# Sliding-window attention feeding a feed-forward layer: later batches loaded in runs of four tokens, V on another queue, and a re-ordered first batch

## The chip, the cores and the metric

The kernel runs on one core of one Trainium2 chip. The metric is device time in microseconds (us). A run is called fast or slow: a slow run is one more than 1.5% above the fastest run of the same kernel.

## The reference

Eight batches of eight heads attend over 576 tokens with head size 64, each token to its neighbours within 32 positions. The result, 4608 rows of 512, goes through a two-layer feed-forward block.

```python
scores = q @ k.T / sqrt(64); mask = |i - j| <= 32          # q, k, v: (8, 8, 576, 64) float32
x = softmax(where(mask, scores, -1e9)) @ v                  # to (4608, 512)
h = relu(x @ w_in)                                          # w_in (512, 2048)
out = (s * h * h + b) @ w_out                               # w_out (2048, 512)
```

## The kernel before

The whole program is built as a graph of tasks. A planner with a table of estimated costs puts the tasks into one fixed order per engine queue (PE, ACT, DVE, Pool, and SP, which issues DMAs). On the chip each queue runs strictly in that order, with semaphore waits, so a task that waits for its input holds up everything behind it in its queue.

For batches 2 to 7, q and k come in by token: partition = token, and for each head 64 floats, so every contiguous run in memory is 256 bytes. DVE casts them to bf16 and a DMA transpose puts the head dimension on the partitions.

```python
def chunk(b, t0, n, key):                       # called for n = 256, 256, 64 tokens of each batch
    nx, np_ = (2, 128) if n == 256 else (1, n)
    for name in "qk":
        add("sp", [... e.dma_start(STG[si][0:np_, x*512:x*512+512].rearrange("p (h d) -> p h d", h=H),
              src_of[name][b, :, t0+128*x : ..., :].rearrange("h p d -> p h d")) for x in range(nx)], ...)
        add("dve", ... tensor_copy(NAT, STG) ...)                        # cast
        add("sp", [... e.dma_start(dst[:, :, ...], NAT[0:np_, x, :], transpose=True) for x in range(nx)], ...)

def load_v(b, t, key, waits=()):                # 128 tokens; runs of 256 bytes too
    add("sp", lambda e: e.dma_start(VST[0:n, t, :, :], v[b, :, 128*t:128*t+n, :].rearrange("h p d -> p h d")), ...)
def cast_v(b, t, key, eng, slack): ...          # eng is Pool for batches 1 to 7

def finish(b, u):                               # a unit is 128 tokens: reciprocal, normalise into XN, then
    if b < XPE: ...                             # XPE = 3: x transposed by PE, copied to XT by ACT
    else: ...                                   # x transposed by a DMA from XN to XT
# [cut: scores on PE, exponent on ACT, mask on DVE, weighted V on PE; the feed-forward stages s1 (w<-xt,win), s2 (o<-wout,gt)]
```

s1 and s2 are the dense work: 128x512 matmuls, four of which take about 0.86 us. Between s1 and s2, ACT applies relu and DVE squares (`gt<-r`).

The softmax here doesn't subtract the row's maximum and nothing guards it: scores larger than these inputs give would overflow.

## Time and profile before

| | before |
|---|---|
| time, median of the first 3 runs | 366.87 us (366.63 to 369.42) |
| span of the profiled run | 369.4 us |
| mean granted PE clock | 0.949 |
| PE idle, 100 to 270 us (40 us and 50 us windows) | 27.4 us |
| DMA share of 16 engines, 80 to 240 us | 0.78 |

These are lines of the page of the kernel before: the span, busy time and share of PE, PEld (weight loads), DVE, ACT and Pool; then rows of 40 slices, each digit a slice's busy share in tenths; the SP-issued DMA queue (packets, MB, share of 16 engines); and the chain of work that ended last, by engine.

```profile
span 369.4 us, 8204 instructions
PE 319.2 (86%) x3452; PEld 169.3 (46%) x3452; DVE 176.7 (48%) x376; ACT 141.7 (38%) x217; POOL 42.6 (12%) x64
...
PE   3679997979699569674999997979699999999996
...
PEclk9999999899889889995999998998989999999999
DMA  8999999967995974697669875797744111001012
...
q1 hardware_dynamic: 150624, 56.19, 66.1%
...
PE 54%; DMA 18%; SPq 17%; DVE 6%; issue 3%; ACT 1%; POOL 0%; DVEq 0%
```

PE is the busiest engine, but between the 7th and the 30th slice its row has holes, and the clock row dips at many of them. The Trainium skill ("TensorE: Matmul & The Clock Gate", Part 1) says that an idle PE falls back to half its clock. The trace agrees: after a wait of 7.8 us that ended at 171.4 us, four dense matmuls took 1.82 us instead of 0.86. No other engine is near full either, so the chain of waits must be read. It spends 17% of the span in SP's queue (SPq) and 18% in DMA flight.

From the chain of the kernel before in order of time (start, us, what):

```profile
121.27 0.90 SPq L421
...
125.90 1.14 SPq L463
...
127.09 2.00 SPq L463
...
129.13 1.88 SPq L588
...
131.05 2.36 DMA xt<-xn
...
133.44 0.70 DVE xn L572
```

Six load issues of 0.9 to 2.0 us, three of which are shown, stand in SP's queue ahead of one xt transpose, which frees the buffer that the next normalisation (`xn`) waits for. That is head-of-line blocking.

How fast the DMAs move seems to depend on the runs; these two windows differ in more than that, and `runs_256` below tests it. Columns: the window, busy us (and count) of PE, PEld, DVE, ACT, POOL, then clock, DMA share, GB/s; the first window moves weights in 2 KB runs, the second mostly q, k and v in 256-byte runs.

```profile
23.00:27.00 4.00, 3.51 (x83) 2.96 (x84) 2.06 (x6) 0.84 (x2) 1.04 (x1) 1.00 1.03 370
120.00:130.00 10.00, 6.08 (x66) 2.70 (x65) 5.41 (x12) 2.98 (x5) 1.61 (x2) 0.83 1.26 221
```

The waits of the kernel before (engine, line, what it waited for; total us, times, longest):

```profile
POOL vb L428 <- DMA vst<-in_v_dram: 199.1, 33, 22.9
...
DVE nat L470 <- DMA stg<-in_q_dram: 29.9, 9, 6.2
...
DVE xn L572 <- DMA xt<-xn: 23.3, 10, 5.3
...
PE avn L550 <- DMA qt<-nat: 7.8, 1, 7.8
```

### The profile page before, as it was taken

What the parts mean: (1) busy time and instruction counts of PE and PEld (TensorE: products, weight loads), DVE (VectorE), ACT (ScalarE), POOL (GpSimd) and SP (SyncE); (2) the same over time, 40 slices, a digit from 0 to 9 for tenths busy, and PEclk for the clock granted to TensorE, in tenths of its full rate; (3) what the DMA queues carried; (4) which work ended last, traced back from release to release, by engine and by line L of the source; (5) the groups of instructions that cost most, each with busy time, mean ns of one, the idle gap of its engine ahead of it and who ended that gap; (6) DMA issues with size and microseconds to landing.
All of it is one profiled execution on the core that took longest, in us unless ns stands there. A gap on an engine that the chain in (4) does not pass through costs nothing.

```text
span 369.4 us, 8204 instructions
## 1 busy us (share of the span) xinstructions
PE 319.2 (86%) x3452; PEld 169.3 (46%) x3452; DVE 176.7 (48%) x376; ACT 141.7 (38%) x217; POOL 42.6 (12%) x64
## 2 busy tenths in 40 slices
PE   3679997979699569674999997979699999999996
PEld 3459886645344223332444443434244444444442
DVE  3557875556444543442556256355265453333321
ACT  3555463456236232431444433523234443333300
POOL 3223551200110110011100110010100000000000
PEclk9999999899889889995999998998989999999999
DMA  8999999967995974697669875797744111001012
GB/s 263 245 358 357 245 287 225 158 128 151 205 155 135 226 151 96 134 219 146 142 115 199 180 167 122 148 187 161 155 112 121 46 44 67 28 30 58 31 57 85
DMA packets 150661, 56.71 MB, mean 154 GB/s; under 512 B 137312, under 2 KB 142432, under 8 KB 150624
## 3 DMA queue, kind: packets, MB, share of 16 engines
q1 hardware_dynamic: 150624, 56.19, 66.1%
q8 instruction: 27, 0.44, 0.6%
q14 instruction: 10, 0.08, 0.1%
HBM read 36.70 MB, written 9.44 MB: 125 GB/s over the span
## 4 chain that ended last, share of the span: by engine, by line
PE 54%; DMA 18%; SPq 17%; DVE 6%; issue 3%; ACT 1%; POOL 0%; DVEq 0%
PE o L730 25%; PE w L711 23%; SPq L463 6%; DMA xt<-xn 4%; DMA stg<-in_moe_w_out_dram 3%; DMA stg<-in_q_dram 3%; PE avn L550 3%; SPq L421 3%; SPq L588 2%; SPq L475 2%; DMA out_dram<-outs 2%; DMA vst<-in_v_dram 2%; DMA qt<-nat 2%; PE sc L498 2%; DVE ex L523 1%
## 5 line engine op out<-in xcount | busy, mean ns | idle before, releaser
L711 PE MATMUL w<-xt,win 128*128 128x512 bf16 (+2 forms) x704 | 152.4, 354 | 1.4 <-DMA xt<-xn 1.4
L730 PE MATMUL o<-wout,gt 128*128 128x512 bf16 (+1 forms) x640 | 151.7, 371 | 1.6 <-DVE outs L743 1.4
L718 ACT ACTIVATE r<-w 128x512 bf16<-128x512 f32 x144 | 85.9, 597 | 137.5 <-PE w L711 98.2
L720 DVE TENSOR_TENSOR gt<-r 128x512 bf16<-128x512 bf16 x144 | 62.6, 444 | 69.3 <-ACT r L718 69.1
L730 PEld LDWEIGHTS o<-wout,gt 128*128 128x128 bf16 x640 | 62.9, 101 | 67.6 <-issue 7.5
L711 PEld LDWEIGHTS w<-xt,win 128*128 128x128 bf16 x704 | 64.0, 102 | 61.2 <-issue 7.7
L519 ACT ACTIVATE ex<-sc 128x1024 bf16<-128x1024 f32 (+3 forms) x45 | 41.3, 927 | 43.9 <-PE avn L550 39.5
L550 PE MATMUL avn<-vb,ex 64*64 64x65 bf16 x1024 | 24.6, 205 | 30.4 <-DVE ex L523 13.4
L428 POOL CAST vb<-vst 128x512 bf16<-128x512 f32 (+1 forms) x37 | 25.2, 681 | 199.4 <-DMA vst<-in_v_dram 199.1
L470 DVE CAST nat<-stg 128x1024 bf16<-128x1024 f32 (+1 forms) x36 | 21.6, 599 | 42.6 <-DMA stg<-in_q_dram 29.9
L550 PEld LDWEIGHTS avn<-vb,ex 64*64 64x64 bf16 x1024 | 16.5, 114 | 46.3 <-DVE ex L523 17.1
L743 DVE SCALAR_TENSOR_TENSOR outs<-o,sb,cvec 128x512 f32<-128x512 f32 (+1 forms) x40 | 27.7, 692 | 20.3 <-PE o L730 12.0
L572 DVE TENSOR_TENSOR xn<-avn,rec 128x512 bf16<-128x512 f32 (+1 forms) x36 | 24.8, 688 | 23.9 <-DMA xt<-xn 23.3
L523 DVE TENSOR_TENSOR ex<-ex,mask 128x1024 bf16<-128x1024 bf16 (+3 forms) x45 | 28.7, 644 | 3.9 <-ACT ex L519 3.5
L498 PE MATMUL sc<-qt,kt 64*64 64x128 bf16 x576 | 20.8, 238 | 2.3 <-DVE kt L454 1.1
L498 PEld LDWEIGHTS sc<-qt,kt 64*64 64x64 bf16 x576 | 13.9, 118 | 3.9 <-ACT ex L519 1.6
L570 DVE RECIPROCAL rec<-avn 128x8 f32<-128x8 f32 (+1 forms) x36 | 7.2, 201 | 15.1 <-PE avn L550 14.9
L582 ACT COPY xt<-avn 128x384 bf16<-128x384 bf16 (+1 forms) x11 | 5.8, 524 | 12.1 <-PE avn L579 12.1
L579 PE MATMUL avn<-ident,xn 128*128 128x128 bf16 (+1 forms) x44 | 4.8, 240 | 4.2 <-DVE xn L572 4.0
L448 PE MATMUL w<-ident,nat 64*64 64x64 bf16 x72 | 2.8, 240 | 6.2 <-ACT nat L441 4.5
L410 POOL CAST wout<-stg 128x1024 bf16<-128x1024 f32 x6 | 6.4, 1062 | 8.9 <-DMA stg<-in_moe_w_out_dram 8.9
L442 DVE CAST nat<-stg 128x576 bf16<-128x576 f32 x8 | 4.1, 508 | 5.7 <-DMA stg<-in_k_dram 5.7
(47 smaller groups left out, 70.3 us busy)
## 6 DMA issues: line engine op xcount, KB each, us to landing
vst<-in_v_dram SPq DMA_DIRECT2D x32, 256.0 KB, 5.2
out_dram<-outs SPq DMA_DIRECT2D x32, 256.0 KB, 2.3
stg<-in_q_dram SPq DMA_DIRECT2D x24, 256.0 KB, 4.2
stg<-in_k_dram SPq DMA_DIRECT2D x24, 256.0 KB, 4.9
stg<-in_moe_w_in_dram SPq DMA_DIRECT2D x8, 512.0 KB, 8.4
stg<-in_moe_w_out_dram SPq DMA_DIRECT2D x8, 512.0 KB, 9.1
stg<-in_q_dram SPq DMA_DIRECT2D x8, 288.0 KB, 5.9
stg<-in_k_dram SPq DMA_DIRECT2D x8, 288.0 KB, 6.2
```

Source lines behind the costliest of these rows:

```text
L428: (lambda e: e.tensor_copy(VB[slot][0:n, t, :, 0:D], VST[0:n, t, :, :])),
L463: add("sp", [lambda e, si=si, name=name, x=x: e.dma_start(STG[si][0:np_, x * 512:x * 512 + 512].rearrange("p (h d) -> p h d", h=H), src_of ...
L498: fns = [lambda e, pr=pr, j=j, hp=hp: e.matmul(SC[64 * (j % 2):64 * (j % 2) + 64, hp, pr * 128:pr * 128 + 128], lhsT=KT[slot][64 * hp:64 * ...
L519: add("act", lambda e, dst=dst, src=src: e.activation(dst, src, AF.Exp, bias=0.0, scale=0.125), 190 + 0.833 * 512 * len(hs), reads=[("SC", ...
L523: add("dve", lambda e, flat=flat, mask=mask: e.tensor_tensor(flat, flat, mask, ALU.mult), 130 + 0.53 * 512 * len(hs), reads=[("E", ei, hp) ...
L550: return [lambda e: e.matmul(av[64 * x:64 * x + 64, h, 0:D + 1], lhsT=buf[64 * g:64 * g + 64, h % 2, h // 2, c:c + 64], rhs=VB[slot][64 * ...
L572: add("dve", lambda e: e.tensor_tensor(XN[xi][0:p1, :].rearrange("p (a c) -> p a c", a=H), av[0:p1, :, 0:D], REC[ri][0:p1, :].rearrange("p ...
L711: add("pe", [lambda e, g=g, kc=kc: e.matmul(wt[:, g, :], lhsT=WIN_BF[:, kc, (f0 + g) * 128:(f0 + g + 1) * 128], rhs=XT[:, kc, t0 % XR:t0 % ...
L718: add("act", lambda e: e.activation(rt, wt, AF.Relu, bias=0.0, scale=1.0), 190 + 0.833 * 512, reads=[("W", wb)], writes=[("R1", rb)], key=key)
L720: add("dve", lambda e: e.tensor_tensor(GT[gs][:, f0:f0 + ng, g0:g0 + nt], rt, rt, ALU.mult), 130 + 0.53 * 512, reads=[("R1", rb)], writes= ...
L730: add("pe", [lambda e, fc=fc: e.matmul(O[:, ob, 0:cn], lhsT=GT[gs][:, fc, g0:g0 + 128], rhs=WOUT_BF[:, fc, c0:c0 + cn], start=(fc == 0), s ...
L743: add("dve", lambda e: e.scalar_tensor_tensor(OUTS[us][:, 0:cn], O[:, ob, 0:cn], SB128[:, 0:1], CVEC[:, c0:c0 + cn], ALU.mult, ALU.add), 2 ...
```

## The change

Its intent, part by part: q and k of batches 2 to 7 come as four tokens per partition, so a run is 1 KB, one load and one large transpose replace several; V of those batches is issued from Pool's queue, to relieve SP; loads are placed a batch ahead; V casts go to DVE; six output buffers instead of three, and a third buffer for `xn`; and in batch 0 the scores and exponents are made head pair by head pair as the pairs land, with the first weights loaded between the V tiles.

```diff
-PACE = ((-1,-1,0,0,1,1),(-1,-1,0,0,1,1),(-1,-1,0,0,1,1))
+PACE = ((-1,-1,-1,-1),)*3
-EV2 = ("pool", "pool", "pool", "pool", "pool")
+EV2 = ("dve",) * 5
-NSTG, NNAT, NEX, NXN, NR1, NOUT, XR = 9, 4, 5, 2, 3, 3, 2048
+NSTG, NNAT, NEX, NXN, NR1, NOUT, XR = 8, 6, 5, 3, 3, 6, 2048
 # load_v
-            add("sp", lambda e: e.dma_start(VST[0:n, t, :, :], ...
+            add("sp" if b < 2 else "pool", lambda e: e.dma_start(VST[0:n, t, :, :], ...
 # chunk: n = 512 and 64; np_ = n // 4
+                add("sp", ... e.dma_start(stg.rearrange("p (h c) -> p h c", h=H),
+                    src_of[name][b, :, t0:t0 + n, :].rearrange("h (p i) d -> p h (i d)", i=4)), ...
+                add("dve", ... tensor_copy(nat.rearrange("p (i h d) -> p h i d", ...), stg.rearrange("p (h i d) -> p h i d", ...)), ...
+                add("sp", ... e.dma_start(dst.rearrange("p i a s -> p (i a) s"), nat, transpose=True), ...
+                # k comes out as token = 4*s + i: Pool puts it back in order, 128 tokens at a time
+                        add("pool", ... tensor_copy(KT[slot][...].rearrange("p a (s i) -> p a s i", i=4),
+                            KTR[slot][...].rearrange("p i a s -> p a s i")), ...
 # q stays in that order; the exponent reads the scores with a stride and puts them back
 # batch 0: first_scores(pr) after each k pair; ORDER0 = V0, W_in 0, V1, V2, V3, W_in 1, V4, W_in 2, W_in 3
 # [cut: buffer views, resource names, the planner's cost figures]
```

More of the change, by code (lines that the diff above doesn't have):

```diff
@@ L20 @@
 VW = 66
+QB = 176
+ORDER0 = (0, 8, 1, 2, 3, 9, 4, 10, 11)
+WINE = ("pool", "pool", "pool", "pool")
 SWITCH = 215.0
@@ L299, in bass_sliding_window_symmetric__then__act_starrelu_kernel @@
         XT = sb((128, NPAIR, XR), BF16, "xt")
-        STG = [sb((128, 2 * DM), F32, "stg") for _ in range(NSTG)]
-        NAT = [sb((128, 2, DM), BF16, "nat") for _ in range(NNAT)]
-        QT = [sb((128, NPAIR, S + 2 * WIN), BF16, "qt") for _ in range(2)]
+        STGS = sb((128, NSTG, 2 * DM), F32, "stg")
+        STG = [STGS[:, i, :] for i in range(NSTG)]
+        NATS = sb((128, NNAT, 2 * DM), BF16, "nat")
+        NAT = [NATS[:, i, :] for i in range(NNAT)]
+        KTR = [sb((128, 4, NPAIR, 144), BF16, "ktr") for _ in range(2)]
+        QTS = [sb((128, 16, QB), BF16, "qt") for _ in range(2)]
+        QT = [t.rearrange("p a c -> p (a c)")[:, 0:NPAIR * (S + 2 * WIN)].rearrange("p (a c) -> p a c", a=NPAIR)
+              for t in QTS]
         KT = [sb((128, NPAIR, S), BF16, "kt") for _ in range(2)]
@@ L305, in bass_sliding_window_symmetric__then__act_starrelu_kernel @@
         VB = [sb((128, NUNIT, H, VW), BF16, "vb") for _ in range(2)]
-        EX = [sb((128, 2, NPAIR, 128), BF16, "ex") for _ in range(NEX)]
+        EXS = sb((128, NEX, 2, NPAIR, 128), BF16, "ex")
+        EX = [EXS[:, i, :, :, :] for i in range(NEX)]
         MASK = sb((128, 128), BF16, "mask")
@@ L407, in load_weights @@
             add("sp", lambda e: e.dma_start(stg, src), 600.0, writes=[("STG", si)], key=key,
-                dma=("l", 16, 85.0) if which == "in" else ("l", 32, 48.0))
+                dma=("l", 16, 92.0) if which == "in" else ("l", 32, 50.0))
             land[which, i, x] = g.tasks[-1]
@@ L420, in load_v @@
             n = min(128, S - 128 * t)
-            add("sp", lambda e: e.dma_start(VST[0:n, t, :, :], v[b, :, 128 * t:128 * t + n, :].rearrange("h p d -> p h d")),
-                640.0, writes=[("VST", t)], key=key, dma=("l", n // 2, 18.0), waits=waits)
+            add("sp" if b < 2 else "pool",
+                lambda e: e.dma_start(VST[0:n, t, :, :], v[b, :, 128 * t:128 * t + n, :].rearrange("h p d -> p h d")),
+                640.0 if b < 2 else 1000.0, writes=[("VST", t)], key=key,
+                dma=("l", n // 2, 20.0) if b < 2 else ("v", n // 32, 300.0), waits=waits)
             land["v", b, t] = g.tasks[-1]
@@ L438, in load_pair @@
                 src_of[name][b, 2 * pr:2 * pr + 2, :, :].rearrange("h (p i) d -> (h p) (i d)", i=ROWS)),
-                600.0, writes=[("STG", si)], key=load_key, dma=("l", 8, 94.0))
-            nat = NAT[ni].rearrange("p a c -> p (a c)")[:, 0:576]
+                600.0, writes=[("STG", si)], key=load_key, dma=("l", 8, 112.0))
+            nat = NAT[ni][:, 0:576]
             add(eng, (lambda e: e.copy(nat, STG[si][:, 0:576])) if eng == "act" else
@@ L455, in load_pair @@
                 writes=[({"q": "QT", "k": "KT"}[name], slot, x, pr) for x in range(NTILE)], key=key)
-        def chunk(b, t0, n, key):
-            slot = b % 2
-            nx, np_ = (2, 128) if n == 256 else (1, n)
-            for name in "qk":
-                si, ni = take("stg", NSTG), take("nat", NNAT)
-                add("sp", [lambda e, si=si, name=name, x=x: e.dma_start(
-                    STG[si][0:np_, x * 512:x * 512 + 512].rearrange("p (h d) -> p h d", h=H),
-                    src_of[name][b, :, t0 + 128 * x:t0 + 128 * x + np_, :].rearrange("h p d -> p h d"))
-                    for x in range(nx)],
-                    600.0 * nx, writes=[("STG", si)], key=key - 20.0,
-                    waits=[paced(b, PACE[min(b, 4) - 2][t0 // 128 + "qk".index(name)])],
-                    dma=("l", n // 2, 18.0))
-                add("dve", lambda e, si=si, ni=ni: e.tensor_copy(
-                    NAT[ni].rearrange("p x c -> p (x c)")[0:np_, 0:512 * nx], STG[si][0:np_, 0:512 * nx]),
-                    110 + 0.53 * 512 * nx,
-                    reads=[("STG", si)], writes=[("NAT", ni)], key=key, slack=3000.0)
-                dst = QT[slot][:, :, WIN:WIN + S] if name == "q" else KT[slot]
-                add("sp", [lambda e, ni=ni, dst=dst, x=x: e.dma_start(
-                    dst[:, :, t0 + 128 * x:t0 + 128 * x + np_], NAT[ni][0:np_, x, :], transpose=True)
-                    for x in range(nx)],
-                    1250.0 * nx * np_ / 128, reads=[("NAT", ni)],
-                    writes=[({"q": "QT", "k": "KT"}[name], slot, x, pr) for x in pieces(t0, t0 + n, 64) for pr in range(NPAIR)],
-                    key=key + 0.1, dma=("t", n // 4, 22.0))
@@ new lines, in q_window, with q_later, chunk @@
+        def q_window(b, pr, j):
+            if b < 2:
+                return QT[b][:, pr, 64 * j:64 * j + 128]
+            return q_later(b)[:, :, pr, 16 * j + 8:16 * j + 40]
+        def q_later(b):
+            return QTS[b % 2].rearrange("p (i a) s -> p i a s", i=4)
+        def chunk(b, t0, n, key, names="qk"):
+            slot, np_, s0 = b % 2, n // 4, t0 // 4
+            if b < 4 and t0 == 0 and "q" in names:
+                for c0, x in ((0, 0), (160, WIN + S)):
+                    add("pool", lambda e, c0=c0: e.memset(QTS[slot][:, :, c0:c0 + 16], 0.0), 400,
+                        writes=[("QTZ", slot, x)] + [("QT", slot, x, pr) for x in range(NTILE) for pr in range(NPAIR)],
+                        key=key - 20.0)
+            for name in names:
+                ring["stg"] += ring["stg"] % 2
+                ring["nat"] += ring["nat"] % 2
+                si, _ = take("stg", NSTG), take("stg", NSTG)
+                ni, _ = take("nat", NNAT), take("nat", NNAT)
+                stg = STGS[0:np_, si:si + 2, :].rearrange("p x c -> p (x c)")
+                nat = NATS[0:np_, ni:ni + 2, :].rearrange("p x c -> p (x c)")
+                stgr, natr = [("STG", si), ("STG", si + 1)], [("NAT", ni), ("NAT", ni + 1)]
+                add("sp", lambda e, stg=stg, name=name: e.dma_start(
+                    stg.rearrange("p (h c) -> p h c", h=H),
+                    src_of[name][b, :, t0:t0 + n, :].rearrange("h (p i) d -> p h (i d)", i=4)),
+                    500.0, writes=stgr, key=key - 20.0,
+                    waits=[paced(b, PACE[min(b, 4) - 2][2 * (t0 > 0) + "qk".index(name)])], dma=("l", np_ // 2, 50.0))
+                add("dve", lambda e, stg=stg, nat=nat: e.tensor_copy(
+                    nat.rearrange("p (i h d) -> p h i d", h=H, i=4), stg.rearrange("p (h i d) -> p h i d", h=H, i=4)),
+                    110 + 0.53 * 2048, reads=stgr, writes=natr, key=key, slack=3000.0)
+                dst = q_later(b)[:, :, :, 16 + s0:16 + s0 + np_] if name == "q" else KTR[slot][:, :, :, s0:s0 + np_]
+                xs = pieces(t0, t0 + n, 64)
+                add("sp", lambda e, nat=nat, dst=dst: e.dma_start(
+                    dst.rearrange("p i a s -> p (i a) s"), nat, transpose=True),
+                    1900.0, reads=natr,
+                    writes=[("QT", slot, x, pr) for x in xs for pr in range(NPAIR)] if name == "q" else [("KTR", slot, t0)],
+                    key=key + 0.1, dma=("t", np_, 22.0))
+                if name == "k":
+                    land["kt", b, t0] = g.tasks[-1]
+                    for c in range(t0, t0 + n, 128):
+                        w = min(128, t0 + n - c)
+                        add("pool", lambda e, c=c, w=w: e.tensor_copy(
+                            KT[slot][:, :, c:c + w].rearrange("p a (s i) -> p a s i", i=4),
+                            KTR[slot][:, :, :, c // 4:(c + w) // 4].rearrange("p i a s -> p a s i")),
+                            100 + 4.8 * w, reads=[("KTR", slot, t0)],
+                            writes=[("KT", slot, x, pr) for x in pieces(c, c + w, 64) for pr in range(NPAIR)],
+                            key=key + 3.0, slack=2000.0)
@@ L500, in qk_part @@
                 lhsT=KT[slot][64 * hp:64 * hp + 64, pr, 64 * j:64 * j + 64],
-                rhs=QT[slot][64 * hp:64 * hp + 64, pr, 64 * j:64 * j + 128], start=True, stop=True)
+                rhs=q_window(b, pr, j)[64 * hp:64 * hp + 64], start=True, stop=True)
                 for pr in range(NPAIR) for j in tiles(u) for hp in hps]
@@ L518, in exp_mask @@
                 flat = dst.rearrange("p i a c -> p (i a) c")
-                add("act", lambda e, dst=dst, src=src: e.activation(dst, src, AF.Exp, bias=0.0, scale=0.125),
+                if b > 1:
+                    flat_src = src.rearrange("p i a c -> p (i a) c").rearrange("p a (i c) -> p a c i", i=4)
+                    flat_dst = flat.rearrange("p a (c i) -> p a c i", i=4)
+                else:
+                    flat_src, flat_dst = src, dst
+                add("act", lambda e, dst=flat_dst, src=flat_src: e.activation(dst, src, AF.Exp, bias=0.0, scale=0.125),
                     190 + 0.833 * 512 * len(hs), reads=[("SC", hp) for hp in hs],
-                    writes=[("E", ei, hp) for hp in hs], key=key)
+                    writes=[("E", ei, hp, pr) for hp in hs for pr in range(NPAIR)], key=key)
                 mask = MASK[0:n, :].rearrange("p (one c) -> p one c", one=1).to_broadcast((n, 4 * len(hs), 128))
                 add("dve", lambda e, flat=flat, mask=mask: e.tensor_tensor(flat, flat, mask, ALU.mult),
-                    130 + 0.53 * 512 * len(hs), reads=[("E", ei, hp) for hp in hs] + [("MASK", p0) for p0 in (0, 64)],
-                    writes=[("E", ei, hp) for hp in hs], key=key)
+                    130 + 0.53 * 512 * len(hs), reads=[("E", ei, hp, pr) for hp in hs for pr in range(NPAIR)] + [("MASK", p0) for p0 in (0, 64)],
+                    writes=[("E", ei, hp, pr) for hp in hs for pr in range(NPAIR)], key=key)
         def av_banks(b, u):
-            if b < 2 and u % 2:
-                return (O, W)[b], [("OW"[b], 0), ("OW"[b], 1)]
-            return AVN, [("AVN", 0), ("AVN", 1)]
+            name = ("SC", "O", "AVN", "SC", "O")[u] if b == 0 else "W" if b == 1 and u % 2 else "AVN"
+            return {"SC": SC, "O": O, "AVN": AVN, "W": W}[name], [(name, 0), (name, 1)]
         def av_part(b, u):
@@ L557, in av_part, with finish @@
                    for n in (0, 1)]
-            reads = [("E", ei, hp) for hp in (0, 1)] + ([("E", pi, hp) for hp in (0, 1)] if u > 0 else [])
+            reads = [("E", x, hp, pr) for x in ({ei, pi} if u > 0 else {ei}) for hp in (0, 1) for pr in range(NPAIR)]
             reads += [("V", slot, x) for x in ({u, u - 1} if u > 0 else {u})] + [("VBO", slot)]
             return fns, reads, res, 340.0
-        def finish(b, u):
-            key = due(b, u)
+        def finish(b, u, key=None):
+            key = due(b, u) if key is None else key
             n = b * NUNIT + u
@@ L604, in pe_part, with first_scores @@
             return t
-        def first_units(b):
-            for u in range(NUNIT):
-                for hp in (0, 1):
-                    pe_part(due(b, u), sc=qk_part(b, u, (hp,)))
-                exp_mask(b, u, ((0,), (1,)))
-                land["av", b, u] = pe_part(due(b, u), av=av_part(b, u))
-                finish(b, u)
+        def first_scores(pr):
+            name, bank = (("SC", SC), ("O", O))[pr % 2]
+            fns = [lambda e, j=j, hp=hp: e.matmul(
+                bank[64 * (j % 2):64 * (j % 2) + 64, hp, 64 * (j - j % 2):64 * (j - j % 2) + 128] if j < 8 else
+                AVN[0:64, hp, pr * 128:pr * 128 + 128],
+                lhsT=KT[0][64 * hp:64 * hp + 64, pr, 64 * j:64 * j + 64],
+                rhs=QT[0][64 * hp:64 * hp + 64, pr, 64 * j:64 * j + 128], start=True, stop=True)
+                for j in range(NTILE) for hp in (0, 1)]
+            key = -30.0 + pr
+            add("pe", fns, SWITCH + 330.0, reads=[("QT", 0, x, pr) for x in range(NTILE)] +
+                [("KT", 0, x, pr) for x in range(NTILE)] + [("QTZ", 0, 0), ("QTZ", 0, WIN + S)],
+                writes=[(name, 0), (name, 1), ("AVN", 0), ("AVN", 1)], key=key, slack=300.0)
+            for u0, n in ((0, 4),) if pr < NPAIR - 1 else ((0, 2), (2, 2)):
+                src = bank[:, :, 128 * u0:128 * (u0 + n)].rearrange("p h (u c) -> p h u c", c=128)
+                first_exp(EXS[:, u0:u0 + n, :, pr, :], src, 128, [(name, 0), (name, 1)],
+                          [("E", u, hp, pr) for u in range(u0, u0 + n) for hp in (0, 1)], key)
+            if pr == NPAIR - 1:
+                first_exp(EXS[0:64, 4, :, :, :].rearrange("p (one h) a c -> p (one a) h c", one=1),
+                          AVN[0:64, :, :].rearrange("p h (a c) -> p h a c", c=128), 64, [("AVN", 0), ("AVN", 1)],
+                          [("E", 4, hp, x) for x in range(NPAIR) for hp in (0, 1)], -24.5)
@@ new lines, in first_exp @@
+        def first_exp(dst, src, np_, sc, res, key):
+            n = dst.shape[1]
+            add("act", lambda e: e.activation(dst.rearrange("p u h c -> p h u c"), src, AF.Exp, bias=0.0, scale=0.125),
+                190 + 0.833 * 256 * n, reads=sc, writes=res, key=key)
+            mask = MASK[0:np_, :].rearrange("p (x y c) -> p x y c", x=1, y=1).to_broadcast((np_, n, 2, 128))
+            add("dve", lambda e: e.tensor_tensor(dst, dst, mask, ALU.mult),
+                130 + 0.53 * 256 * n, reads=res + [("MASK", p0) for p0 in (0, 64)], writes=res, key=key)
@@ L615, in bass_sliding_window_symmetric__then__act_starrelu_kernel, with first_units @@
+        def first_units():
+            for u in range(NUNIT):
+                land["av", 0, u] = pe_part(-25.0 + u, av=av_part(0, u))
+                finish(0, u, -25.0 + u)
         last = []
@@ L628, in close @@
                 finish(*bu)
-        b0_banks = [(("W", 0), W[:, 0, :]), (("O", 0), O[:, 0, :]), (("W", 1), W[:, 1, :]), (("O", 1), O[:, 1, :])]
+        b0_banks = [(("W", 0), W[:, 0, :]), (("W", 1), W[:, 1, :])]
         b1_banks = [(("SC", 0), SC[:, 0, :]), (("SC", 1), SC[:, 1, :])]
@@ L644, in qk @@
                             load_pair(0, name, pr, -60.0 + 0.1 * pr, nxt(), b0_banks, eng, 200.0)
+                            if name == "k":
+                                first_scores(pr)
                         else:
@@ L650, in w @@
                 for x in (0, 1):
-                    load_weights(which, i, x, nxt(), (("pool", "act"), ("pool", "dve"))[i % 2][x])
+                    load_weights(which, i, x, nxt(), WINE[i])
             def w_out(x):
@@ L657, in attention @@
             qk(0)
-            for t in range(NUNIT):
-                load_v(0, t, nxt())
-                cast_v(0, t, -55.0 + t, EV0[t], 300.0)
-            first_units(0)
-            for i in range(4):
-                w("in", i)
+            for t in ORDER0:
+                if t < 8:
+                    load_v(0, t, nxt())
+                    cast_v(0, t, -28.0 + t, EV0[t], 300.0)
+                else:
+                    w("in", t - 8)
+            first_units()
             for i, src in enumerate((moe_s, moe_b)):
@@ L678, in attention @@
             for b in range(2, B):
-                for x, (t0, n) in enumerate(((0, 256), (256, 256), (512, 64))):
-                    chunk(b, t0, n, due(b, max(0, t0 // 128 - 1)) - 20.0)
-                    for t in ((0, 1), (2, 3), (4,))[x]:
-                        load_v(b, t, due(b, max(0, t0 // 128 - 1)) - 39.9, waits=[paced(b, PACEV[min(b, 4) - 2][t])])
-                        cast_v(b, t, due(b, max(0, t0 // 128 - 1)) - 4.0, EV2[t], 3000.0)
-                    for u in ((0,), (1, 2), (3, 4))[x]:
-                        unit(b, u)
-                        yield b * S + (unit_rows(u - 1)[1] if u else 0)
+                for t0, n in ((0, 512), (512, 64)):
+                    chunk(b, t0, n, due(b, 0) - 24.0)
+                for t in range(NUNIT):
+                    load_v(b, t, due(b, t) - 35.0, waits=[paced(b, PACEV[min(b, 4) - 2][t])] + ([land["kt", 2, 0]] if b == 2 else []))
+                    cast_v(b, t, due(b, t) - 4.0, EV2[t], 3000.0)
+                for u in range(NUNIT):
+                    unit(b, u)
+                    yield b * S + (unit_rows(u - 1)[1] if u else 0)
             close()
```

## The prediction

> **What bounds it now.**
> 1. 0-24 us: batch 0's attention. The first dense matmul (w<-xt,win) starts at 24.2 us in the timeline. DMA is saturated to about 65 us (slices).
> 2. 24-270 us: PE starved in turns. Summing PE idle over 10- and 20-us windows between 60 and 280 us gives about 35 us; the granted clock falls to 0.66-0.91 after most gaps (mean 0.949, some 19 us lost). The chain of waits there alternates between the SP queue issuing (17% of the span), DMA landings (18%), and an in-order DVE stuck behind a cast or an output buffer. Examples: 83-98 us, q and k loads of 4.8 and 5.0 us while nat casts hold DVE; 121-131 us, six SP load issues in a row before one xt transpose; 157-171 us, the same, ending in PE's longest wait (7.8 us, on qt<-nat).
> 3. 270-367 us: no later loads, PE back to back; 4 dense 512-column matmuls per 0.865 us, one attention unit about 0.75 us.
>
> Floor from phase 3's rates. At 99.4 us of the profiled run 960 dense matmuls remain (207 us), some 28 units (21 us), and a 3 us drain: 331 us, against 369.4. So about 38 us is lost after 99 us. Likewise 16 us before it.
>
> **What the change does.**
> - q/k of batches 2-7: 256 B runs become 1 KB. 256 B loads saturate the DMAs at 221 GB/s (120-130 us), 2 KB weight rows at 370 (23-27 us). Estimate for 1 KB 350: 2.36 MB a batch takes 6.7 us instead of 10.5. The Trainium skill ("DMA: Bandwidth & Descriptors", Why small descriptors are slow) has a fixed cost per packet; the trace agrees in direction.
> - SP queue per batch: 20 load/transpose issues become 8, and 5 V issues leave for Pool. At 1.1-1.3 us each (larger transposes maybe 2) SP falls from about 38 to about 20 us per batch, which takes PE 35 us.
> - Added: V casts to DVE (30 x 0.43 = 13 us), k reordering on Pool (30 x about 0.7 us), strided exponent reads on ACT (1.02 us, likely unchanged), software descriptors for V on Pool (about 1 us an issue, guessed). DVE is 48% busy, Pool 12%: off the path. The skill ("SBUF — State Buffer", Who interferes with whom) warns that DVE's two-port operations starve a Pool queue's descriptor writing; V is issued some 30 us early, so I expect it hidden.
> - Six output buffers remove DVE waits on out_dram<-outs (8.3 us; 58-61 and 74-78 us lie on the chain).
> - Start: weights amid V and early exponents start dense work about 4 us earlier; DMA still delivers w_out at about 33 us, so only 2-3 us remain.
>
> **Sum.** Of 38 us after 99 us I recover about 24, the rest staying as DMA bunching; of 16 us before it about 6; start 2. 367 - 32 = **335 us, range 322-352**. Chances: faster 0.92, same 0.06, slower 0.02.
>
> **Right if:** mean clock about 0.98; SPq's share of the chain under 8%; PE idle in 100-270 us under 10 us; q/k load packets a quarter as many; first dense matmul at about 20 us. **Wrong steps would show as:** DVE long waiting on vst (V late by Pool), large transposes costing much more than 2 us of SP issue, dense start not earlier.
>
> **What would make it wrong:** V's software descriptors slow (over 7 us a tile), blocking Pool's k reordering; DMA transposes being the true DMA load; DVE casts blocking the squaring that PE waits for.

## More of the kernel before

Pool's 199 us of waiting for V is harmless, for Pool has nothing else to do. DVE's waits for q and for xt are not: behind them in DVE's queue stand the squarings that the dense work needs.

## The result

The time was 348.68 us (median of 4 runs, 344.67 to 351.46) against 367.54 us (4 runs): inside the predicted range of 322 to 352, but 13.7 us above the predicted 335. Ratios here are the mean time of one kernel's fast runs over that of the other's in the same rounds, so they are not quite the ratio of the quoted medians. This one is 0.9393 (95% interval 0.9315 to 0.9471). The changed kernel spreads more than the one before; the two runs at 351 us count as slow.

The page of the changed kernel:

```profile
span 344.5 us, 8110 instructions
...
PE   3679998998488999895999996999999999999994
...
PEclk9999999999698999997899999999999999999999
DMA  7999989979961899599979997996212110100021
...
q1 hardware_dynamic: 76416, 49.10, 58.5%
q0 software_dynamic: 2208, 7.08, 11.9%
...
PE 61%; DMA 18%; issue 7%; DVE 7%; POOL 4%; ACT 1%; SPq 1%; POOLq 0%
```

The chain now has SPq at 1% instead of 17%, as intended. PE idle between 100 and 270 us fell from 27.4 to 11.2 us (under 10 was predicted), and the clock rose to 0.975. But the DMA row is at 9 for longer than before. Multiplying the shares by the span: before, 66.1% of 369.4 is 244 us of all 16 engines; after, 58.5% plus 11.9% (q0, the Pool queue) of 344.5 is 243 us. The packets grew, yet their times add up to as much. (Packet times overlap: the window at 120 us above has a share of 1.26. So these sums measure the load on the DMAs, not pure work.)

The chain of the changed kernel between 76 and 101 us, and its waits:

```profile
76.42 12.26 DMA ktr<-nat
...
88.73 3.61 POOL kt L512
...
93.17 4.94 DMA vst<-in_v_dram
...
98.47 2.58 DVE nat L498
```

```profile
POOL kt L512 <- DMA ktr<-nat: 59.9, 7, 19.1
...
POOL vst L431 <- PE avn L591: 45.1, 11, 10.3
...
DVE vb L439 <- DMA vst<-in_v_dram: 16.5, 10, 3.1
...
PE avn L591 <- DVE ex L565: 10.0, 3, 5.8
...
DVE xn L613 <- DMA xt<-xn: 4.1, 1, 4.1
...
PE avn L591 <- POOL kt L512: 4.1, 2, 2.6
```

A k transpose took 12.3 us to land, one reordering copy on Pool then 3.6 us, and V 4.9 us. PE's wait of 7.8 us for a q transpose is gone; it still waits for the mask on DVE (`ex`, 10.0 us; 13.4 before), and 4.1 us for Pool's copies. DVE's waits for xt fell from 23.3 to 4.1 us; in their place it waits 16.5 us for V. The second line tells much of why V comes late: Pool's V issues wait for PE's weighted V of the batch before (the pacing `PACEV`, which the change left alone). The first V of each batch was issued at 71.1, 92.3, 117.0, 144.4, 179.6 and 216.4 us, and its cast started at 79.6, 96.9, 125.9, 152.8, 190.2 and 226.7: 4.6 to 10.6 us later, where the prediction had counted on some 30. The copies' line (min/median/max ns) shows that they are far from the 0.7 us that was predicted:

```profile
L512 POOL COPY kt<-ktr x30: 611/1145/3612, 73.9 to 240.7; 128x512 bf16<-128x512 bf16 x24, 128x256 bf16<-128x256 bf16 x6
```

### The profile page after: what moved, and what is told of

The parts are those of the page before. It is cut to its first block, busy times and chain, and to the rows that moved or that the text cites. A ratio compares the mean times of both kernels' runs of the same rounds, so it can differ in the third digit from the quotient of the medians.

```text
span 344.5 us, 8110 instructions
## 1 busy us (share of the span) xinstructions
PE 309.4 (90%) x3452; PEld 166.9 (48%) x3452; DVE 208.7 (61%) x388; ACT 139.2 (40%) x211; POOL 92.4 (27%) x102
## 3 DMA queue, kind: packets, MB, share of 16 engines
q1 hardware_dynamic: 76416, 49.10, 58.5%
q0 software_dynamic: 2208, 7.08, 11.9%
## 4 chain that ended last, share of the span: by engine, by line
PE 61%; DMA 18%; issue 7%; DVE 7%; POOL 4%; ACT 1%; SPq 1%; POOLq 0%
PE o L801 28%; PE w L782 25%; DMA ktr<-nat 6%; DMA vst<-in_v_dram 4%; DMA xt<-xn 4%; PE avn L591 3%; DMA stg<-in_moe_w_in_dram 2%; POOL kt L512 2%; DVE nat L498 2%; PE sc L535 2%; DMA stg<-in_k_dram 2%; DVE ex L565 1%; POOL vst L431 1%; PE o L824 1%; DVE xn L613 1%
## 5 line engine op out<-in xcount | busy, mean ns | idle before, releaser
L801 PE MATMUL o<-wout,gt 128*128 128x512 bf16 (+1 forms) x640 | 147.1, 363 | 2.3 <-DVE gt L791 1.4
L791 DVE TENSOR_TENSOR gt<-r 128x512 bf16<-128x512 bf16 x144 | 71.0, 501 | 64.8 <-ACT r L789 64.6
L512 POOL COPY kt<-ktr 128x512 bf16<-128x512 bf16 (+1 forms) x30 | 37.3, 1242 | 61.2 <-DMA ktr<-nat 59.9
L561 ACT ACTIVATE ex<-sc 128x1024 bf16<-128x1024 f32 (+1 forms) x35 | 35.8, 1022 | 38.7 <-PE avn L591 34.3
L431 POOL DMA_DIRECT2D vst<-in_v_dram x30 | 26.7, 893 | 48.7 <-PE avn L591 45.1
L498 DVE CAST nat<-stg 128x2048 bf16<-128x2048 f32 (+1 forms) x24 | 31.0, 1307 | 10.0 <-DMA qt<-nat 4.2
L565 DVE TENSOR_TENSOR ex<-ex,mask 128x1024 bf16<-128x1024 bf16 (+1 forms) x35 | 26.1, 744 | 2.2 <-ACT ex L561 1.1
L613 DVE TENSOR_TENSOR xn<-avn,rec 128x512 bf16<-128x512 f32 (+1 forms) x34 | 23.3, 684 | 4.8 <-DMA xt<-xn 4.1
L439 DVE CAST vb<-vst 128x512 bf16<-128x512 f32 (+1 forms) x32 | 14.5, 466 | 16.7 <-DMA vst<-in_v_dram 16.5
L535 PE MATMUL sc<-qt,kt 64*64 64x128 bf16 x504 | 15.5, 223 | 0.0
L419 POOL CAST win<-stg 128x1024 bf16<-128x1024 f32 x8 | 8.4, 1056 | 10.6 <-DMA stg<-in_moe_w_in_dram 10.6
```

Of the source, the lines that this page charges most:

```text
L431: lambda e: e.dma_start(VST[0:n, t, :, :], v[b, :, 128 * t:128 * t + n, :].rearrange("h p d -> p h d")),
L498: add("dve", lambda e, stg=stg, nat=nat: e.tensor_copy(nat.rearrange("p (i h d) -> p h i d", h=H, i=4), stg.rearrange("p (h i d) -> p h i ...
L512: add("pool", lambda e, c=c, w=w: e.tensor_copy(KT[slot][:, :, c:c + w].rearrange("p a (s i) -> p a s i", i=4), KTR[slot][:, :, :, c // 4: ...
L535: fns = [lambda e, pr=pr, j=j, hp=hp: e.matmul(SC[64 * (j % 2):64 * (j % 2) + 64, hp, pr * 128:pr * 128 + 128], lhsT=KT[slot][64 * hp:64 * ...
L561: add("act", lambda e, dst=flat_dst, src=flat_src: e.activation(dst, src, AF.Exp, bias=0.0, scale=0.125), 190 + 0.833 * 512 * len(hs), rea ...
L565: add("dve", lambda e, flat=flat, mask=mask: e.tensor_tensor(flat, flat, mask, ALU.mult), 130 + 0.53 * 512 * len(hs), reads=[("E", ei, hp, ...
```

## The experiments

The theories, by the letters that the expectations use: P says that the gain comes from the packet size, which lowers the time of the DMA engines; its rival Q says that it comes from unloading SP's queue. (S and H are explained where they occur.) For what V on Pool costs there are four: D, packets from Pool's queue are costlier; G, casts on DVE starve Pool's descriptor writing; I, two queues share the engines, so that urgent transposes lose their turn; K, V's issues and the reordering copies collide on Pool.

Rounds alternate with the kernel before on the same chip. Of the six parts listed above, three were undone singly, the runs of four were tried without most of the others, one cost was measured by itself, and combinations followed. Each edit except the one to run length also changes a cost or a task that the planner sees, so the fixed orders change with it; that stays a caveat of every such comparison.

| kernel | median us | ratio to before | 95% interval |
|---|---|---|---|
| after_again (the changed kernel) | 350.13 | 0.9426 | 0.9349 to 0.9503 |
| runs_256 | 363.79 | 0.9871 | 0.9824 to 0.9917 |
| v_on_sp | 340.29 | 0.9218 | 0.9174 to 0.9261 |
| old_start | 350.76 | 0.9526 | 0.9483 to 0.9570 |
| copy_on_act | 366.78 | 0.9897 | 0.9843 to 0.9951 |
| v_sp_copy_act | 345.21 | 0.9388 | 0.9347 to 0.9430 |
| only_runs | 337.80 | 0.9202 | 0.9156 to 0.9249 |
| v_sp_xpe8 | 336.47 | 0.9149 | 0.9097 to 0.9201 |
| v_sp_vcast_pool | 332.75 | 0.9050 | 0.9008 to 0.9093 |
| v_sp_xpe8_vcast_pool | 329.82 | 0.8889 | 0.8856 to 0.8922 |
| v_sp_vcast_pool_xpe5 | 327.37 | 0.8862 | 0.8809 to 0.8915 |

Medians are over all runs, ratios over fast ones. A hundredth of a ratio is about 3.7 us, taking before as 368 us. The kernels ran in four jobs on four chips, each beside the kernel before; kernels of different jobs are compared through these ratios. The slow mark cuts off half of after_again's runs, which scatter without a clear gap. By medians over all runs v_on_sp gains 9.8 us on it instead of 7.7, runs_256 loses 13.7 instead of 16.4, and old_start 0.6 instead of 3.7: single steps are uncertain by some 3 us.

### after_again: the yardstick

No edit.

> The changed kernel, unaltered, as the yardstick of this job. All theories: ratio to the kernel before 0.935 to 0.95, with runs spread between 344 and 352 us as in the four runs already seen.

The ratio came out at 0.9426, as expected. The spread was wider than expected: three of its six runs (350.6 to 354.9 us) count as slow.

### runs_256: the same instructions, 256-byte runs

```diff
-stg.rearrange("p (h c) -> p h c", h=H),     src...rearrange("h (p i) d -> p h (i d)", i=4)
+stg.rearrange("p (i h d) -> p i h d", ...), src...rearrange("h (p i) d -> p i h d", i=4)
-tensor_copy(nat.rearrange("p (i h d) -> p h i d"), stg.rearrange("p (h i d) -> p h i d"))
+tensor_copy(nat, stg)
```

> One part undone: q and k of batches 2 to 7 still come in one DMA of 512 tokens with four tokens per partition, the same instructions in the same order, but each token's 256 bytes land apart, so every packet is 256 B instead of 1 KB (the cast then reads contiguously). Theory P: the q and k loads take 10.5 instead of 6.7 us of all the DMA engines per batch, DMA is saturated in 120 to 240 us, so 10 us or more slower (ratio 0.965 or more). Theory Q: the issues are the same, so within 4 us of the changed kernel (ratio up to 0.95).

This is the cleanest experiment: every engine's instructions stand in the same order as in the changed kernel, only the shapes of these loads and casts differ. The casts took as long (1.22 us in the median in both), so the loads are what differs: DVE's casts waited 19.0 us for them instead of 1.9. It lost 16.4 us of the gain (0.9871 against 0.9426). The DMA queue lines of runs_256 (span 361.2 us), then of after_again (span 347.2 us):

```profile
q1 hardware_dynamic: 117888, 49.10, 63.9%
q0 software_dynamic: 2208, 7.08, 10.4%
```

```profile
q1 hardware_dynamic: 76416, 49.10, 58.8%
q0 software_dynamic: 2208, 7.08, 11.9%
```

That is 74.3% of 361.2 = 268 us against 70.7% of 347.2 = 245 us. The prediction had put the q and k loads at 6.7 us a batch instead of 10.5, so 23 us over six batches; the difference is 23 us. Theory P is right about this part; that the two agree to the microsecond is partly luck, for packet times overlap and the run time moved by 16.4 us. The Trainium skill ("DMA: Bandwidth & Descriptors", Why small descriptors are slow) gives a fixed cost per packet as the reason; these runs show the effect, not the mechanism.

### v_on_sp: V back on the SP queue

```diff
-add("sp" if b < 2 else "pool", lambda e: e.dma_start(VST...
+add("sp", lambda e: e.dma_start(VST...
```

> One part undone: V of batches 2 to 7 is issued by the SP queue again, all else as in the changed kernel. Theory Q (the gain came from freeing the SP queue and the in-order engines from waits): five issues of about 1.1 us come back to a queue that is then about 26 us full per batch of 35 to 39 us, so 3 to 8 us slower than the changed kernel (ratio 0.95 to 0.96). Theory P (the gain came from larger packets, that is DMA engine time): no change, ratio within 0.005 of the changed kernel, or even faster if software-made descriptors cost DMA time.

Theory Q's forecast of 3 to 8 us lost failed: with five more issues per batch in SP's queue the kernel was 7.7 us faster (0.9218 against 0.9426). So the move of V to Pool was a cost on balance, not a gain. What fewer and larger issues of q and k bring is not tested by this. The DMA line of v_on_sp (span 339.0 us):

```profile
q1 hardware_dynamic: 104544, 56.18, 67.4%
```

67.4% of 339.0 is 228 us, 17 us less than with V on Pool. One line each on the q and k transposes (us from issue to landing, min/median/max), first after_again, then v_on_sp:

```profile
DMA to landing us min/median/max: 2.4/6.4/18.7
```

```profile
DMA to landing us min/median/max: 2.3/4.5/6.9
```

With V on Pool the median landing was 6.4 us and the worst 18.7; with V on SP 4.5 and 6.9. DVE waited for V just as long (18.7 us, shown below), so that wait is no mark of the Pool queue. Its packets also verify the prediction's count: with V on the same queue in both kernels, those of 512 bytes to 2 KB rise by 13,824, exactly a quarter of the 55,296 that q and k of six batches took in 256-byte runs.

### copy_on_act and v_sp_copy_act: why does V on Pool cost time?

```diff
-add("pool", lambda e, c=c, w=w: e.tensor_copy(KT[slot]...
+add("act",  lambda e, c=c, w=w: e.copy(KT[slot]...
```

The second also has the edit of v_on_sp.

> V still on the Pool queue, only the k reordering copies (37 us of Pool time in all) move from Pool to ACT. V on SP was about 10 us faster than V on Pool; this asks why. Theory K (on Pool the V issues and the k copies block each other, and the copies and DVE stretch each other): with the copies gone most of that comes back, ratio 0.92 to 0.93. Theory D (software-made V packets cost more DMA engine time, 41 us of all 16 engines against about 25 for the same bytes by the SP queue): DMA unchanged, ratio stays 0.935 to 0.945.

> V on the SP queue and the k copies on ACT, so Pool does nothing after 60 us. If the copies on Pool still hold DVE or PE up (PE waited 5.6 us for them with V on SP), 3 to 6 us faster than V on SP alone: ratio 0.905 to 0.915. If not, 0.92 within 0.005.

Both missed their expectations. The ACT copies made things worse, by 17 us with V on Pool and 6 us with V on SP. The waits of v_sp_copy_act show why:

```profile
ACT kt L511 <- DMA ktr<-nat: 18.4, 6, 5.7
...
PE w L781 <- ACT r L788: 12.2, 5, 5.7
```

In ACT's in-order queue the copy waits for the k transpose, behind it waits relu, and PE waits for relu. Pool was the better place for the copies: nothing but V's issues stands behind them there. The pair still answers its question in part. With the copies away from Pool, V on Pool costs more than before (0.9897 against 0.9388, 19 us), not less, so a collision with the copies on Pool (theory K) is not needed for the cost, and cannot be all of it. In copy_on_act the q and k transposes landed after 8.9 us in the median and 21.6 at worst, against 4.7 and 8.2 in v_sp_copy_act, and DVE waited 29.0 us for V instead of 17.7.

### v_alone: the disputed cost by itself

A kernel of six phases on 256 KB V tiles and 128x2048 transposes. Its output is wrong, which doesn't matter for the time.

```python
SP: 16 V tiles;  Pool: 16 V tiles;  Pool: 16 V tiles while DVE casts;  SP: 8 transposes;
SP: 8 x (1 transpose, 2 V tiles);  SP: 8 transposes while Pool issues 16 V tiles       # each phase waits for the last
```

> A measurement, not the computation: the result is wrong on purpose (zeros). Six phases, each waiting for the last: 16 V tiles of 256 KB by the SP queue; the same by the Pool queue; the same by Pool while DVE casts f32 to bf16 all the time; eight 128x2048 DMA transposes alone; the eight transposes with 16 V tiles, all by SP; the eight transposes by SP with 16 V tiles by Pool. Theory D (a software-made V load itself costs more DMA time): the Pool phase moves 4.2 MB at 170 GB/s or less against 220 or more by SP, alone as well. Theory G (DVE's casts starve the descriptor writing): alone as fast as SP, slower by 1.5 times or more beside the casts. Theory I (interleaving: the second queue takes turns with the transposes and makes them late): phases one to three alike, and in the last phase the transposes take clearly longer to land than in the phase where SP issues all.

The phases as windows (us; DVE and POOL busy; clock; DMA share; GB/s):

```profile
core 0: us, DVE busy (x) POOL busy (x), PEclk, DMA share, GB/s
5.70:27.10 21.40, 0.00 (x0) 0.00 (x0) 1.00 1.15 196
27.10:51.90 24.80, 0.00 (x0) 14.14 (x16) 1.00 0.78 169
52.20:82.00 29.80, 29.80 (x22) 24.09 (x16) 1.00 0.55 141
85.25:107.25 22.00, 0.00 (x0) 0.00 (x0) 1.00 1.03 191
107.25:148.40 41.15, 0.00 (x0) 0.00 (x0) 1.00 1.01 204
148.40:192.70 44.30, 0.00 (x0) 14.00 (x16) 1.00 1.07 189
```

Sixteen V tiles took 21.4 us by SP, 24.8 by Pool, and at most 29.8 by Pool beside casts. In the last two the DMA share was only 0.78 and 0.55: the engines lacked work, they were not slower. From 29 to 46 us the Pool phase moved 220 GB/s; the loss came at its ends, the sixteenth tile being issued 7.9 us after the fifteenth. So theory D's 170 GB/s came true (169), but not for its reason: alone, packets from Pool take no more DMA time (0.78 of 24.8 us is 19 us, 1.15 of 21.4 is 25).

In the kernels they do: the same 7.08 MB took 41 us of packet time by Pool (2,208 packets, 11.9% of 344.5 us) and 24 us by SP (28,128 packets, the difference between v_on_sp and after_again). Whether that is work or waiting for other packets, no run tells.

Starvation by casts (theory G) is seen here, with Pool's issues at 1.51 instead of 0.88 us, although the phase grew by 1.2 times and not by the expected 1.5; in the changed kernel Pool's V issues took 0.88 us in the median and 1.51 at most, so there it can explain little. The Trainium skill ("SBUF — State Buffer", A bandwidth-pool intuition that's wrong) has 620 ns growing to 3100 ns for one such DMA beside a DVE copy; here an issue grew 1.7 times.

The transposes of phase five (all by SP), then of phase six (V by Pool; its first line gives the issues, min/median/max ns):

```profile
DMA to landing us min/median/max: 4.5/5.2/5.4
```

```profile
L31 SPq DMA_TRANSPOSE tr<-nat x8: 1323/3261/19316, 148.4 to 187.9; - x8
...
DMA to landing us min/median/max: 4.5/6.0/24.4
```

The two phases took 41.2 and 44.3 us in total, but with V on the other queue one transpose landed only after 24.4 us instead of 5.4 at worst, and one issue was stuck in SP for 19.3 us. This is what theory I expects: two queues share the 16 engines, and the more urgent one loses its turn. It rests on one transpose of eight in one run (the medians are 5.2 and 6.0 us), and V's own landings grew too, from 4.0 to 15.1 us in the median. The Trainium skill ("DMA: Bandwidth & Descriptors", Queues, rings and completion order) describes the engines as taking turns between queues by packet. The trace does not contradict that (V's packets by Pool are some 13 times larger than by SP, by the counts above, so a turn of V would be long), but it does not show the turns. Sixteen V tiles at once is a heavier load than the kernel's two to four.

### old_start: the first batch as before

```diff
-ORDER0 = (0, 8, 1, 2, 3, 9, 4, 10, 11)      # V0, W_in 0, V1, V2, V3, W_in 1, V4, ...
+ORDER0 = (0, 1, 2, 3, 4, 8, 9, 10, 11)
-first_scores(pr) after each k pair; weight casts all on Pool
+scores, exponents and masks by unit; weight casts on Pool, ACT, DVE
```

> One part undone: batch 0's scores by unit, first V before the first weights, the weight casts shared with ACT and DVE, as in the kernel before; later batches as in the changed kernel. The dense start moved only from 24.2 to 22.4 us, so theory Q and theory P both expect 0 to 3 us slower (ratio 0.938 to 0.95). Theory S (the start gave most of the gain) expects 10 us or more slower (ratio 0.965 or more).

0.9526 against 0.9426: the new start is worth 3.7 us by the ratios, slightly more than expected, and 0.6 us by the medians. The first dense matmul came 1.2 us earlier than in this run's own profile (22.4 against 23.5 us, a slow run; 24.2 in the kernel before). The intervals overlap, so a gain is likely but not shown; theory S is ruled out.

### only_runs: the runs of four without most other parts

The edits of v_on_sp and old_start, with these:

```diff
-EV2 = ("dve",) * 5
+EV2 = ("pool",) * 5
-NSTG, NNAT, NEX, NXN, NR1, NOUT, XR = 8, 6, 5, 3, 3, 6, 2048
+NSTG, NNAT, NEX, NXN, NR1, NOUT, XR = 8, 6, 5, 3, 3, 3, 2048
```

> One part alone: runs of four tokens with the large transposes, the k copies on Pool and the re-ordered exponents, as in the changed kernel; V on SP, V casts on Pool, three output buffers and the first batch as in the kernel before. Theory P (packet size is the gain): ratio 0.92 to 0.945, as good as the whole change. Theory Q (waits, buffers, queue): 0.96 or more, most of the gain missing.

It was better than the whole change: 0.9202, 8.2 us below it. The runs of four with what was kept beside them (the large transposes, loads a batch ahead, the third buffer for `xn`) give all of the net gain; the other parts together take some back. It cannot be told from this run alone how much is due to packet size, how much to fewer issues (8 instead of 20 loads and transposes per batch), and how much to the earlier loads or that buffer.

### v_sp_vcast_pool: what the V casts on DVE cost

The edits of v_on_sp and `EV2 = ("pool",) * 5`.

> V on SP and the V casts on Pool, x still transposed by DMA for batches 3 to 7. Against v_on_sp (ratio 0.922, the same but for the casts on DVE) it gives what the cast's move to DVE cost: theory H (a cast that waits for V in DVE's in-order queue holds up the squaring that PE needs) expects 0.90 to 0.912; if the casts were harmless on DVE, 0.92. Against only_runs (0.920, the same but for three output buffers and the old first batch) it gives what those two parts bring together: old_start says about 1%, so 0.91. Against v_sp_xpe8_vcast_pool (0.889) it gives what the DMA transposes of x cost.

0.9050 against v_on_sp's 0.9218: moving the V casts back to Pool is worth 6.2 us. The wait for V did not go away, it moved to an engine where it harms nobody. First v_on_sp, then v_sp_vcast_pool:

```profile
DVE vb L438 <- DMA vst<-in_v_dram: 18.7, 9, 4.3
```

```profile
POOL vb L438 <- DMA vst<-in_v_dram: 87.6, 23, 14.5
```

18.7 us of waiting on DVE cost more than 87.6 us on Pool. The move also takes some 13 us of cast work off DVE; this run does not separate that from the waits. Against only_runs (0.9202) the new start and the six output buffers together are worth 5.6 us. And 332.75 us is near the 335 that the prediction gave for the whole change.

### v_sp_xpe8, v_sp_xpe8_vcast_pool and v_sp_vcast_pool_xpe5: less for the DMAs

`XPE = 8` (then 5) lets PE transpose x for all batches (then up to batch 4), with ACT's copy cut in two where XT wraps. All three have V on SP; the last two have the V casts on Pool.

> V on SP, and x is transposed by PE and copied by ACT for all batches instead of by DMA for batches 3 to 7. It adds about 25 x 0.39 us = 10 us to PE, and takes 27 DMA transposes off the SP queue and the DMA engines. If the DMA engines still set the pace (share 0.84 in 80 to 240 us), the relief outweighs the cost: ratio 0.90 to 0.92. If PE sets it by now, 4 to 10 us slower than V on SP: 0.93 to 0.95.

> A candidate to beat both kernels: V on SP, x transposed by PE for all batches, and the V casts on Pool as in the kernel before, which takes 13 us of casts from a DVE that is 63% busy. If DVE's order still costs PE time, 1 to 3 us faster than with the casts on DVE: ratio 0.905 to 0.915. If Pool's in-order queue makes the k copies wait for V, slower: 0.92.

> A candidate: as the best so far, but x is transposed by PE only to batch 4, by DMA for 5 to 7. PE runs without idling from 100 us on in the best kernel, so taking 15 units' transposes of 0.39 us off PE gains up to 6 us (ratio 0.872 to 0.885) if the DMAs keep up there; if they do not, 0.89 to 0.90.

v_sp_xpe8 at 0.9149 lies just below v_on_sp, their intervals overlapping. With the casts on Pool the step is clear: 0.8889 (0.905 to 0.915 was expected) against 0.9050, 5.9 us, although PE has more work. PE then runs without idling from 100 to 240 us, so the DMA transposes of x had probably been part of what it waited for. Giving x of batches 5 to 7 back to the DMAs brought 0.8862, within the interval: the hoped-for 6 us did not come. v_sp_vcast_pool_xpe5 at 327.37 us beats the kernel before by 11% and the changed kernel by 6%.

## Why the prediction was right, and where it was off

- **What bounded the kernel: right.** PE starved in turns, with the clock falling after gaps, and the floor reckoned from the dense rate was some 38 us below. The experiments removed 41 us without touching the dense work.
- **Packet size: right in mechanism, and about right in size.** The estimate of 3.8 us of all DMA engines per batch makes 23 us; runs_256 shows 23 us of DMA time and 16.4 us of run time.
- **SP's queue: right as a reading, mis-sized as a lever.** SPq fell to 1% of the chain (predicted under 8%). Fewer, larger issues are part of only_runs' gain, but taking V off SP brought nothing, for v_on_sp is faster with V in it. A named sign of error appeared: the large transposes, put at maybe 2 us of SP's time, took up to 12.5 us each (q, 2.4 in the median) with V on Pool, and at most 4.0 with V on SP.
- **"V is issued some 30 us early, so I expect it hidden": this step failed.** V was issued only 4.6 to 10.6 us before its cast, and its landing (8.6 us median) takes about that long. But DVE waits as long for V that SP issues, so the 7.7 us that the move to Pool cost lie elsewhere, most likely in the transposes, which landed later. The Trainium skill ("DMA: Bandwidth & Descriptors", Issuing engines are not separate DMA queues) says that issuing from several engines saves only issue time; this case agrees (44.3 us for transposes and V from two queues, 41.2 from one), and adds that transposes can land late.
- **"DVE is 48% busy, Pool 12%: off the path": this step failed.** Busy share does not say what an in-order queue blocks. The V casts on DVE cost 6.2 us. The prediction named DVE waiting on vst as a sign of error, and it appeared (16.5 us), though not, as the prediction put it, because Pool was late.
- **k reordering on Pool at 0.7 us: mis-sized.** It took 1.24 us on average (0.61 to 3.61). PE waited 4.1 us for it in all.
- **Start: open in size.** 0.6 to 3.7 us measured, 2 predicted; the dense start at 22.4 us, predicted 20. The output buffers were not measured alone; start and buffers together gave 5.6 us.
- **The sum.** Measured steps: runs of 1 KB 16.4, start and buffers 5.6, V on Pool -7.7, V casts on DVE -6.2; the total of after_again is 21.1 (0.0574 of 368), so about 13 us are left for fewer and larger issues, earlier loads, the third buffer for `xn` and the new order. That remainder was not isolated, and the steps need not add up exactly. The predicted 32 is near the 35 that the change gives without its two harmful parts, and these two (13.9 us) are about the 13.7 by which it missed. The time stayed inside the range because the range was wide: slow runs of after_again reached 354.9, outside it.

Still open: how the cost of V on Pool divides between late transposes, gaps in the descriptor supply and the changed order; why it was 19 us with the copies on ACT but 7.7 us with them on Pool; and whether V issued earlier, by another pacing, would have removed the waits, which no run tried.

## What to carry to other kernels

Before moving work to an idle engine, look at what stands behind it in that engine's in-order queue: a wait of 88 us on Pool cost less than one of 19 us on DVE, and a copy on ACT held up relu and PE. A second DMA queue did not pay here, and urgent transposes landed later beside it; one queue in a planned order was better. When a load is counted as hidden, look in the trace when it is really issued. Larger runs paid here, where the DMAs were saturated, and a change of several parts should be tried part by part, for the runs of four without most other parts beat the whole.

## What the Trainium skill lacked or had wrong

- "DMA: Bandwidth & Descriptors", Issuing engines are not separate DMA queues: it says what a second queue saves, not what it can cost. Here V on Pool made the kernel 7.7 us slower, and in v_alone the worst transpose landing rose from 5.4 to 24.4 us.
- The same page, DMA Transpose: it gives no time for an SBUF-to-SBUF transpose. Eight of 128x2048 bf16 (4.2 MB) took 22.0 us, 2.75 us each, 191 GB/s, and with V at 256-byte runs between them the two nearly added up (41.2 us against 21.4 + 22.0). The 261 GB/s for transposes in its table under Latency and other measured facts were not reached.
- The same page, SWDGE vs HWDGE vs iDMA: it does not say how many loads from Pool can be outstanding. In all three Pool phases fifteen 256 KB V tiles were issued steadily, and the sixteenth came 3.3 to 17.6 us later, so alone 16 tiles reached 169 GB/s against 196 by SP.
- "SBUF — State Buffer", A bandwidth-pool intuition that's wrong: its five-fold stretch of a Pool-issued DMA beside a DVE copy was not seen; issues went from 0.88 to 1.51 us, and the phase grew by at most 1.2 times. The casts here lasted 1.2 to 1.6 us; no run tried longer ones.
- "GPSIMD Engine Reference" has no time for a strided bf16 `tensor_copy` (its per-element costs are for kernels written for the Q7 cores): 512 elements per partition (256 in six of thirty) took 0.61 to 3.61 us on Pool, 1.24 on average.
